# A squared-ReLU MLP kernel: small loads on other queues, transposes in merged PSUM banks, and a warm-up in four column tiles

## The chip, the cores and the metric

The kernel runs on one core of one Trainium2 chip. The metric is the device time of one execution in microseconds (us), as a median over several executions. "Span" is the time from the first to the last instruction in the profile; the device time is the span plus about 1.7 to 2.2 us. TensorE is called PE, its weight loads PEld, VectorE DVE, ScalarE ACT, GpSimd POOL, and SP is the engine that issues most DMAs.

## The reference

```python
B, S, D, F = 1, 2048, 576, 4608          # all bf16
def reference(x, w1, b1, w2, b2):
    h = jnp.einsum("bsd,df->bsf", x, w1) + b1
    r = jnp.where(h > zero, h, zero)
    h = r * r
    out = jnp.einsum("bsf,fd->bsd", h, w2) + b2
    return out
```

## The kernel before

The 2048 rows of x are worked in four blocks of 512. The first matmul contracts over D = 576, which is four full 128-row chunks and one of 64. The kernel deals with this in two ways. Four of the 36 column blocks of w1 ("w1n") are computed with full 128-row matmuls plus a 64-row pair ("w1n8"). The other 32 ("w_h" in the profile, w1_h in the code; when loaded, a piece of it is called a w1 chunk here) are computed as pairs of 64-row matmuls, one in the lower half of the array and one in the upper half, at the same time. I call this the row-tiled part.

x has to reach PE transposed. For blocks 1 to 3 a DMA transposes it; for block 0 there is no time for that, so PE transposes it into PSUM (the memory, divided into banks, that PE writes), and DVE and ACT copy it out, while full-array work on w1n is interleaved. Half 0 is the first 256 rows of the block, half 1 the rest. All of the change is in these first 10 us, the head. Cut to what matters (cuts are marked "# ..."):

```python
    # warm-up: matmuls on constants while the first loads fly
    WARM = [512] * 6 + [128]
    for i, n in enumerate(WARM):
        keep(nc.tensor.matmul(wps[:, 0:n], lhsT=ones[:, 0:P], rhs=ones[:, 0:n], start=True, stop=True))
    # ... loads: x tiles and w1n
    load_x(nc.sync, 0)
    load_x(nc.scalar, 1)
    load_w1n(nc.sync, 0)
    load_x(nc.scalar, 2)
    load_w1n(nc.sync, 1)
    load_x(nc.sync, 3)
    for k in range(2, NK):
        load_w1n(nc.sync, k)
    # ... b1 and b2's column by GpSimd
    nc.gpsimd.dma_start(out=b1_rows[0:NFT, :], in_=b1.rearrange("(ft p) -> ft p", p=P))
    # ... block 0: transposes, copies out of PSUM (DVE and ACT alternate), full-array matmuls
                for j in range(2):
                    for k in range(NK):
                        x_transpose(j, k)
                for j in range(2):
                    x_transpose(j, NK)
                x_copies(0)
                part(0, 0)
                for k in range(NK + 1):
                    x_transpose(2, k)
                part(0, 1)
                part(0, 2)
                for k in range(NK + 1):
                    x_transpose(3, k)
                x_copies(1)
                dup_windows(0)
                part(0, 3)
                part(1, 0)
                make_b1T()
                for k in range(1, NK):
                    part(1, k)
    # ... w1 for the row-tiled part, in the order in which it is needed
    for (j0, j1) in [(0, 1), (1, 2), (2, 4), (4, 6), (6, 8), (8, 10), (10, 12)]:
        load_w1(nc.sync, 0, j0, j1)
        load_w1(nc.sync, 1, j0, j1)
        if j0 == 0:
            load_w1n8(nc.sync, 0)
            load_w1n8(nc.sync, 1)
```

## Time and profile before

| | |
|---|---|
| time, median of 2 runs | 290.95 us (290.84 to 291.06) |
| span of the profiled run (a run of its own, 291.46 us) | 289.6 us; other runs of this kernel had 288.7 to 289.6 |
| PE busy | 285.5 us, 99% |
| row-tiled part starts | 9.85 us (first 64-row pair, which is w1n8's; counted from here below), 10.29 us (first w_h pair) |

The page of the kernel before: the first line gives each engine's busy time, the others the chain of work that ended last.

```profile
PE 285.5 (99%) x2027; PEld 139.9 (48%) x2032; DVE 78.6 (27%) x176; ACT 96.7 (33%) x154; POOL 2.3 (1%) x10
...
PE 98%; DMA 1%; issue 0%; DVE 0%
```

The kernel is PE from end to end, so only gaps in PE's work or slow PE work can be won back. The head, from the timeline of PE (columns: start us, length us, engine, line, operation, output<-inputs, forms, count, and in brackets an idle time before the first of them and what ended it):

```profile
0.78 2.83 PE L63 MATMUL wps<-const-bfloat16-1.0 128*128 128x512 bf16 x7 [0.78 <-PEq L344]
3.77 1.25 PE L149 MATMUL tb<-ident,x_sb 128*128 128x128 bf16 x10 [0.17 <-DMA x_sb<-in_x_dram]
4.87 1.01 PE L227 MATMUL pn<-xTw,w1n 128*128 128x256 bf16 x4
5.68 0.74 PE L149 MATMUL tb<-ident,x_sb 128*128 128x128 bf16 x5
6.21 1.19 PE L227 MATMUL pn<-xTw,w1n 128*128 128x256 bf16 x8
7.24 0.44 PE L149 MATMUL tb<-ident,x_sb 128*128 128x128 bf16 x5
7.51 1.04 PE L227 MATMUL pn<-xTw,w1n 128*128 128x256 bf16 x8
8.39 0.22 PE L166 MATMUL b1T_ps<-ident,b_rows 128*128 128x128 bf16 x1
8.44 1.47 PE L227 MATMUL pn<-xTw,w1n 128*128 128x256 bf16 x12
9.85 0.39 PE L203 MATMUL pn<-xTw,w1n 64*128 64x512 bf16 x1
```

From 3.77 us on, there is no gap. But the same work takes different times: four 256-column matmuls took 1.01 us at 4.87, and eight took 1.04 us at 7.51. PE's clock rises from half to full rate in between. The trace's own clock record puts the rise at 6.51 us in this run.

### The profile page before, as it was taken

The numbers are of one execution on the slowest core, as the hardware profiler recorded it, in microseconds if no ns is written. First come the engines' busy times: TensorE is split into PE (matmuls) and PEld (weight loads), VectorE is DVE, ScalarE is ACT, GpSimd is POOL, SyncE is SP. The second block draws the span as 40 slices with busy tenths as digits, with TensorE's granted clock in tenths as the row PEclk, the third lists the DMA queues.
The fourth block names the chain that finished last, engine by engine and source line by source line (L and its number), as shares of the span: only waits on it lengthen the run. The fifth ranks groups of instructions, "written<-read, shape, count | busy, mean of one in ns | idle before, by whom it ended". The sixth has DMA issues, their size and how long they took to land.

```text
span 289.6 us, 4693 instructions
## 1 busy us (share of the span) xinstructions
PE 285.5 (99%) x2027; PEld 139.9 (48%) x2032; DVE 78.6 (27%) x176; ACT 96.7 (33%) x154; POOL 2.3 (1%) x10
## 2 busy tenths in 40 slices
PE   8999999999999999999999999999999999999996
PEld 5544444444444555555544444444444455555555
DVE  1644554444500200000015444444440001100001
ACT  2566666666500000000027666666670000000000
POOL 3000000000000000000000000000000000000000
PEclk9999999999999999999999999999999999999999
DMA  7999999400001200000000000000000110000000
GB/s 198 221 245 188 308 389 212 92 0 2 0 14 25 52 16 18 16 16 18 16 16 2 1 2 0 2 0 2 0 2 0 36 38 16 16 16 19 33 16 18
DMA packets 31605, 16.52 MB, mean 57 GB/s; under 512 B 15700, under 2 KB 31584, under 8 KB 31584
## 3 DMA queue, kind: packets, MB, share of 16 engines
q1 hardware_dynamic: 31232, 15.91, 22.3%
q10 hardware_dynamic: 288, 0.30, 0.4%
q8 instruction: 16, 0.26, 0.4%
q14 instruction: 5, 0.04, 0.0%
q0 software_dynamic: 64, 0.01, 0.0%
HBM read 11.36 MB, written 2.36 MB: 47 GB/s over the span
## 4 chain that ended last, share of the span: by engine, by line
PE 98%; DMA 1%; issue 0%; DVE 0%
PE ph L188 42%; PE po L289 38%; PE pt L270 11%; PE pn L209 4%; PE pn L227 1%; DMA x_sb<-in_x_dram 1%; PE tb L149 1%; PE ph L190 1%; PE pn L203 1%; DVE o_sb L291 0%; PE b1T_ps L166 0%; PE pn L205 0%
## 5 line engine op out<-in xcount | busy, mean ns | idle before, releaser
L190 PE MATMUL ph<-xTw,w_h 64*128 64x512 bf16 x576 | 124.6, 376 | 0.0
L188 PE MATMUL ph<-xTw,w_h 64*128 64x512 bf16 x576 | 124.6, 376 | 0.0
L289 PE MATMUL po<-w_sb,hT 128*128 128x448 bf16 (+2 forms) x612 | 109.4, 341 | 0.0
L176 ACT ACTIVATE r<-ph,b1T 128x512 bf16<-128x512 f32 x128 | 81.1, 685 | 41.6 <-PE ph L190 41.6
L188 PEld LDWEIGHTS <-w_h 64*128 64x128 bf16 x576 | 54.1, 94 | 68.3
L289 PEld LDWEIGHTS <-hT 128*128 128x128 bf16 x612 | 58.5, 98 | 51.0
L177 DVE TENSOR_TENSOR hT<-r 128x512 bf16<-128x512 bf16 x144 | 61.2, 426 | 75.9 <-ACT r L176 75.5
L190 PEld LDWEIGHTS <-w_h 64*128 64x128 bf16 x576 | 54.1, 94 | 0.0
L291 DVE TENSOR_TENSOR o_sb<-po,b_bc 128x448 bf16<-128x448 f32 (+2 forms) x17 | 10.2, 597 | 125.8 <-PE po L289 125.8
L270 PE MATMUL pt<-hT,w_sb 128*128 128x512 bf16 x142 | 31.3, 379 | 0.1
L176 ACT ACTIVATE r<-pn,b1T 128x512 bf16<-128x512 f32 x16 | 10.3, 688 | 61.0 <-PE pn L205 59.6
L270 PEld LDWEIGHTS <-w_sb 128*128 128x128 bf16 x144 | 14.1, 98 | 17.0
L273 ACT ACTIVATE oT<-pt,b2T 128x512 bf16<-128x512 f32 x4 | 2.8, 688 | 28.3 <-PE pt L270 28.3
L209 PE MATMUL pn<-xTw,w1n 128*128 128x512 bf16 x45 | 10.4, 379 | 0.4 <-issue 0.3
L209 PEld LDWEIGHTS <-w1n 128*128 128x128 bf16 x48 | 4.5, 98 | 6.0 <-issue 0.8
L227 PE MATMUL pn<-xTw,w1n 128*128 128x256 bf16 x32 | 4.6, 295 | 0.0
L63 PE MATMUL wps<-const-bfloat16-1.0 128*128 128x512 bf16 (+1 forms) x7 | 2.8, 582 | 0.8 <-PEq L344 0.8
L227 PEld LDWEIGHTS <-w1n 128*128 128x128 bf16 x32 | 3.3, 107 | 0.5
L156 DVE COPY xTw<-tb 128x256 bf16<-128x256 bf16 x4 | 1.1, 292 | 6.7 <-PE tb L149 6.7
L119 DVE COPY xTw<-xTw 64x2048 bf16<-64x2048 bf16 x4 | 2.8, 690 | 0.2
L120 DVE COPY xTw<-xTw 64x2048 bf16<-64x2048 bf16 x4 | 2.7, 687 | 0.1
L149 PE MATMUL tb<-ident,x_sb 128*128 128x128 bf16 x20 | 2.4, 288 | 0.2 <-DMA x_sb<-in_x_dram 0.2
(23 smaller groups left out, 15.2 us busy)
## 6 DMA issues: line engine op xcount, KB each, us to landing
w_sb<-in_w_dram SPq DMA_DIRECT2D x4, 1296.0 KB, 12.7
w_h<-in_w_dram SPq DMA_DIRECT2D x14, 288.0 KB, 6.2
out_dram<-o_sb SPq DMA_DIRECT2D x15, 112.0 KB, 1.7
w_h<-in_w_dram SPq DMA_DIRECT2D x4, 144.0 KB, 3.5
w1n<-in_w_dram SPq DMA_DIRECT2D x4, 128.0 KB, 3.9
out_dram<-ot SPq DMA_DIRECT2D x4, 128.0 KB, 2.0
x_sb<-in_x_dram ACTq DMA_DIRECT2D x2, 144.0 KB, 2.9
x_sb<-in_x_dram SPq DMA_DIRECT2D x2, 144.0 KB, 3.4
```

The lines of the kernel that those rows point to most:

```text
L63: keep(nc.tensor.matmul(wps[:, 0:n], lhsT=ones[:, 0:P], rhs=ones[:, 0:n], start=True, stop=True))
L149: keep(nc.tensor.transpose(bank[:, slot, qc], xs[:, j, c0:c0 + P], ident[:]))
L176: keep(nc.scalar.activation(out=r[:], in_=bank[:], func=ACT.Relu, bias=b1T[:, ft:ft + 1], scale=1.0))
L177: keep(nc.vector.tensor_tensor(out=hTs[sb][:, ft, :], in0=r[:], in1=r[:], op=ALU.mult))
L188: keep(nc.tensor.matmul(bx[:], lhsT=w1_h[0:H, LO_C[i], jc], rhs=xT[0:H, LO_W[i], :], start=(i == 0), stop=(i == NC - 1)))
L190: keep(nc.tensor.matmul(by[:], lhsT=w1_h[H:P, UP_C[i], jc], rhs=xT[H:P, UP_W[i], :], start=(i == 0), stop=(i == NC - 1)))
L203: keep(nc.tensor.matmul(banks[2 * i][:], lhsT=w1n8[0:H, i, :], rhs=xT[0:H, SPC, :], start=start, stop=stop, skip_group_check=order == "k_o ...
L209: keep(nc.tensor.matmul(banks[g][:], lhsT=w1n[:, k, g * P:(g + 1) * P], rhs=xT[:, O + k, :], start=start, stop=stop))
L227: keep(nc.tensor.matmul(banks[g][:, hc], lhsT=w1n[:, k, g * P:(g + 1) * P], rhs=xT[:, O + k, hc], start=(h == 0 and k == 0), stop=False, s ...
L270: keep(nc.tensor.matmul(pt[:], lhsT=w2_sb[:, ft, DM:D], rhs=hT[:, ft, :], start=(i == 0), stop=(i == NFT - 1)))
L289: keep(nc.tensor.matmul(po[:, 0:d1 - d0], lhsT=hT[:, ft, jj * P:(jj + 1) * P], rhs=w2_sb[:, ft, d0:d1], start=(i == 0), stop=(i == NFT - 1)))
L291: keep(nc.vector.tensor_tensor(out=o_sb[:, d0:d1], in0=po[:, 0:d1 - d0], in1=b2_bc[:, d0:d1], op=ALU.add))
```

## The change

The intent is a shorter head: GpSimd out of the loads (b1, b2), b1 and the small w1 rows on ACT's queue so that SP can issue w1_h sooner, fewer and fuller PSUM banks for the transposes, and a warm-up of four matmuls at a time, each on 32 of the array's columns. The core of the diff:

```diff
-    WARM = [512] * 6 + [128]
-    for i, n in enumerate(WARM):
-        keep(nc.tensor.matmul(wps[:, 0:n], lhsT=ones[:, 0:P], rhs=ones[:, 0:n], start=True, stop=True))
+    CT = P // 4
+    WARM = [512] * 6 + [256]
+    for n in WARM:
+        for c in range(4):
+            keep(nc.tensor.matmul(wps[c * CT:(c + 1) * CT, 0:n], lhsT=ones[:, 0:CT], rhs=ones[:, 0:n],
+                                  start=True, stop=True))
 ...
     load_x(nc.sync, 0)
-    load_x(nc.scalar, 1)
-    load_w1n(nc.sync, 0)
-    load_x(nc.scalar, 2)
-    load_w1n(nc.sync, 1)
-    load_x(nc.sync, 3)
-    for k in range(2, NK):
-        load_w1n(nc.sync, k)
+    for rt in range(1, RT):
+        load_x(nc.scalar, rt)
+    for k0, k1 in [(0, 1), (1, 2), (2, NK)]:
+        load_w1n(nc.sync, k0, k1)
 ...  (the GpSimd loads of b1 and b2 go; ACT's table load and warm activation come here, then:)
+    for h in range(2):
+        load_w1n8(nc.scalar, h)
+    keep(nc.scalar.dma_start(out=b1_rows[0:NFT, :], in_=b1.rearrange("(ft p) -> ft p", p=P)))
 ...  (x_copies: half 0 all on DVE, half 1 on DVE with one double-width copy on ACT)
                 x_copies(0)
+                x_transpose(2)
                 part(0, 0)
-                for k in range(NK + 1):
-                    x_transpose(2, k)
                 part(0, 1)
-                part(0, 2)
-                for k in range(NK + 1):
-                    x_transpose(3, k)
+                x_transpose(3)
                 x_copies(1)
                 dup_windows(0)
+                part(0, 2)
                 part(0, 3)
 ...  (w1n8 leaves SP's queue; b2's column and w2 in three chunks instead of four come late on SP)
```

More of the change, by code (lines that the diff above doesn't have):

```diff
@@ L57 @@
     ps_o = ctx.enter_context(tc.tile_pool(name="ps_o", bufs=4, space=PSUM))
-    wps = ps_o.tile([P, 512], FP32, name="wps", tag="po")
+    wps = ps_h.tile([P, 512], FP32, name="wps", tag="ph")
     ones = nc.const_aps.tensor(1.0, [P, 512], BF16)
-    WARM = [512] * 6 + [128]
-    for i, n in enumerate(WARM):
-        keep(nc.tensor.matmul(wps[:, 0:n], lhsT=ones[:, 0:P], rhs=ones[:, 0:n], start=True, stop=True))
+    CT = P // 4
[4 more added lines that the diff above has]
+                                  start=True, stop=True))
     xs = const.tile([P, RT, D], BF16, name="x_sb")
@@ L72, in load_x, with load_w1n @@
         keep(eng.dma_start(out=xs[:, rt, :], in_=x2[rt * P:(rt + 1) * P, :]))
-    def load_w1n(eng, k):
-        keep(eng.dma_start(out=w1n[:, k, :], in_=w1[k * P:(k + 1) * P, 0:GW]))
+    def load_w1n(eng, k0, k1):
+        src = w1[k0 * P:k1 * P, 0:GW].rearrange("(k p) f -> p k f", p=P)
+        keep(eng.dma_start(out=w1n[:, k0:k1, :], in_=src))
     def load_w1n8(eng, h):
@@ L83, in load_w1 @@
                       in_=w1_v[:, :, GW + h * FH + j0 * P:GW + h * FH + j1 * P]))
+    b1_rows = const.tile([P, P], BF16, name="b1_rows")
+    nc.vector.memset(b1_rows[:], 0.0)
     load_x(nc.sync, 0)
-    load_x(nc.scalar, 1)
-    load_w1n(nc.sync, 0)
-    load_x(nc.scalar, 2)
-    load_w1n(nc.sync, 1)
-    load_x(nc.sync, 3)
-    for k in range(2, NK):
-        load_w1n(nc.sync, k)
+    for rt in range(1, RT):
+        load_x(nc.scalar, rt)
+    for k0, k1 in [(0, 1), (1, 2), (2, NK)]:
+        load_w1n(nc.sync, k0, k1)
     ident = const.tile([P, P], BF16, name="ident")
     make_identity(nc, ident[:])
-    b1_rows = const.tile([P, P], BF16, name="b1_rows")
-    nc.gpsimd.memset(b1_rows[:], 0.0)
-    nc.gpsimd.dma_start(out=b1_rows[0:NFT, :], in_=b1.rearrange("(ft p) -> ft p", p=P))
-    b2_col = const.tile([P, 1], BF16, name="b2_col")
-    nc.gpsimd.dma_start(out=b2_col[:], in_=b2[DM:D].rearrange("(d o) -> d o", o=1))
-    b2T = const.tile([P, 1], FP32, name="b2T")
-    nc.gpsimd.tensor_copy(out=b2T[:], in_=b2_col[:])
     warm = const.tile([P, 1], FP32, name="warm")
     keep(nc.scalar.activation(out=warm[:], in_=nc.const_aps.tensor(0.0, [P, 1], FP32), func=ACT.Relu))
+    for h in range(2):
+        load_w1n8(nc.scalar, h)
+    keep(nc.scalar.dma_start(out=b1_rows[0:NFT, :], in_=b1.rearrange("(ft p) -> ft p", p=P)))
     E3, O, SPC, E = 0, 1, 5, 6
@@ L130 @@
     w2_view = w2.rearrange("(ft p) d -> p ft d", p=P)
-    W2CH = 9
+    W2CH = 12
     def load_w2(c):
@@ L140, with x_transpose @@
     HS = SB // 2
-    tb_po = [ps_o.tile([P, 2, HS], BF16, name="tb", tag="po") for _ in range(2)]
-    tb_ph = [ps_h.tile([P, 2, HS], BF16, name="tb", tag="ph") for _ in range(4)]
-    half_banks = [tb_ph, None]
-    def x_transpose(j, k):
+    tb = [[ps_h.tile([P, 4, HS], BF16, name="tb", tag="ph") for _ in range(2)] for _ in range(2)]
+    PLACE = [(0, 0), (0, 1), (1, 0), (1, 1), (0, 2)]
+    T_ORDER = [0, 1, NK, 2, 3]
+    def x_transpose(j):
         h, q = divmod(j, 2)
-        qc = slice(q * P, (q + 1) * P)
-        bank, slot, c0 = (half_banks[h][k], 0, k * P) if k < NK else (half_banks[h][2], 1, D - P)
-        keep(nc.tensor.transpose(bank[:, slot, qc], xs[:, j, c0:c0 + P], ident[:]))
+        for k in T_ORDER:
+            bank, slot = PLACE[k]
+            c0 = k * P if k < NK else D - P
+            keep(nc.tensor.transpose(tb[h][bank][:, slot, q * P:(q + 1) * P], xs[:, j, c0:c0 + P], ident[:]))
     def x_copies(h):
         hc = slice(h * HS, (h + 1) * HS)
-        for k in range(NK):
-            src = half_banks[h][k][:, 0, :]
-            if k % 2 == 0:
-                keep(nc.vector.tensor_copy(out=xT0[:, O + k, hc], in_=src))
-            else:
-                keep(nc.scalar.copy(out=xT0[:, O + k, hc], in_=src))
-        keep(nc.vector.tensor_copy(out=xT0[:, E3, hc], in_=half_banks[h][2][:, 1, :]))
+        for k in (0, 1):
+            keep(nc.vector.tensor_copy(out=xT0[:, O + k, hc], in_=tb[h][0][:, k, :]))
+        if h == 0:
+            for k in (2, 3):
+                keep(nc.vector.tensor_copy(out=xT0[:, O + k, hc], in_=tb[h][1][:, k - 2, :]))
+        else:
+            keep(nc.scalar.copy(out=xT0[:, O + 2:O + 4, hc], in_=tb[h][1][:, 0:2, :]))
+        keep(nc.vector.tensor_copy(out=xT0[:, E3, hc], in_=tb[h][0][:, 2, :]))
     b1T = const.tile([P, NFT], FP32, name="b1T")
     def make_b1T():
-        b1T_ps = ps_o.tile([P, P], BF16, name="b1T_ps", tag="po")
+        b1T_ps = ps_h.tile([P, P], BF16, name="b1T_ps", tag="ph")
         keep(nc.tensor.transpose(b1T_ps[:], b1_rows[:], ident[:]))
@@ L198, in a_full @@
         for g in range(G):
-            pool, tag = (ps_o, "po") if g < 2 else (ps_h, "ph")
+            pool, tag = (ps_o, "po") if g < 2 or order == "k_outer" else (ps_h, "ph")
             banks.append(pool.tile([P, SB], FP32, name="pn", tag=tag))
@@ L220, in a_full @@
             if order == "k_outer":
-                tb_new = [ps_h.tile([P, 2, HS], BF16, name="tb", tag="ph") for _ in range(2)]
-                half_banks[1] = tb_new + tb_po
                 def part(h, k):
@@ L231, in a_full @@
                 for j in range(2):
-                    for k in range(NK):
-                        x_transpose(j, k)
-                for j in range(2):
-                    x_transpose(j, NK)
+                    x_transpose(j)
                 x_copies(0)
+                x_transpose(2)
                 part(0, 0)
-                for k in range(NK + 1):
-                    x_transpose(2, k)
                 part(0, 1)
-                part(0, 2)
-                for k in range(NK + 1):
-                    x_transpose(3, k)
+                x_transpose(3)
                 x_copies(1)
                 dup_windows(0)
+                part(0, 2)
                 part(0, 3)
@@ L296 @@
         load_w1(nc.sync, 1, j0, j1)
-        if j0 == 0:
-            load_w1n8(nc.sync, 0)
-            load_w1n8(nc.sync, 1)
     load_xT(1)
@@ L303 @@
         load_w1(nc.sync, 1, j0, j1)
+    b2_col = const.tile([P, 1], BF16, name="b2_col")
+    keep(nc.sync.dma_start(out=b2_col[:], in_=b2[DM:D].rearrange("(d o) -> d o", o=1)))
+    b2T = const.tile([P, 1], FP32, name="b2T")
+    nc.gpsimd.tensor_copy(out=b2T[:], in_=b2_col[:])
     keep(nc.sync.dma_start(out=b2_bc[:], in_=b2.partition_broadcast(P)))
-    for c in (0, 2, 1, 3):
+    for c in range(3):
         load_w2(c)
```

## The prediction

> **What bounds it now.** TensorE. The profile's first table has PE busy 285.5 of 289.6 us (99%), and the chain of waits is 98% PE; only x_sb's first load (about 3 us) and the last store lie outside it. From about 10.3 us to 287 us PE issues 512-column matmuls every 0.215 us without gaps, and the diff leaves that part alone (w2 in three chunks instead of four is needed only at 77 us). So only the first 10.3 us can change.
>
> **The head, from the timeline.** Warm-up matmuls start at 0.78 us, 0.427 us apart (half clock), and end near 3.6; x tile 0 lands at 3.72; the transposes start at 3.77; from there PE is dense to the first row-tiled pair at 9.85. In this stretch PE waits for data only 0.2 us. The clock is still low for its first part: 128-column transposes start 0.107 us apart and 256-column matmuls 0.213 us apart until about 6.5 us, then 0.055 and 0.109. At full rate the 21 transposes and 32 matmuls would take 21x0.055+32x0.109 = 4.6 us instead of 6.1. So the most that the head can give is about 1.4 us, 0.5%, and it can be had only by an earlier clock, since PE has no gaps to close.
>
> **What the change does.**
> - GpSimd loads and memset go (POOL is busy 2.3 us, off the chain): worth 0.
> - b1_rows and the small w1 rows move to ScalarE's queue, behind three x issues (0.43 us each), the table load (1.28) and the warm activation (0.2): b1 is issued near 5 us and lands, at the 2.5 to 3.5 us of loads in this stretch, near 7.5 to 8.5. PE's b1 transpose came at 8.39. Just in time; if the clock rises early, a stall of 0 to 0.7 us.
> - Merged banks: half 0's five copies now all run on DVE, 0.29 us each. The first needs the bank's eighth transpose, but five transposes of tile 2 (0.53 us) fill that wait. About 0.
> - w1n chunks 2 and 3 in one load, issued near 2.1 instead of 2.65 us: needed at about 7; no wait, unless PE is earlier.
> - Warm-up as four column tiles. The Trainium skill, "TensorE: Matmul & The Clock Gate", Part 3, reports three column tiles running 2.38 times as fast as in sequence, so I take four as concurrent: the trace already shows the two 64-row tiles starting within 0.01 us of each other. Then the warm-up ends about where it did, 3.6 to 3.9 us. The same page, Part 1, has the clock rise after a busy free-running window of about 3.4 us; the trace agrees loosely (activity from 0.78, rise at 6.5). Four times as many matmuls in a window may count as more activity and raise the clock one window earlier (about 30% by my guess): gain 0.7 to 1.3 us, less the stalls above. Otherwise 0, or a loss of 0.1 to 0.3 us for the drain at the mode switch and the longer last warm-up.
>
> **Predicted: 290.6 us** (0.3*(-1.0) + 0.7*(-0.05), about -0.35), 8 times in 10 between 289.7 and 291.5. Faster by over 2%: 0.01; within 2%: 0.97; slower: 0.02.
>
> **What would show it.** Right: four warm-up matmuls start within some 0.02 us of each other; first transpose at 3.7 to 3.9; the rows part starts between 9 and 10.4 us; its length and everything after unchanged to 0.3 us. Clock: the step at which starts of 256-column matmuls halve their distance, 6.5 before.
>
> **What would make it wrong.** Column tiles run one after the other: 28 warm-up matmuls then last till about 9 us, and the kernel takes some 295 us. Or b1_rows lands after 9 us and PE stalls at its transpose. Or the window's phase differs between executions, and moves either kernel by up to 1 us.

## The result, and the profile after

The changed kernel took 291.24 us (median of 2 runs, 291.12 and 291.35) against 290.95. The ratio is 1.0009, with a 95% interval of 0.9985 to 1.0033. Ratios here are the mean time of one kernel's fast runs over that of the other's of the same rounds, so they are not quite the ratio of the medians quoted. The page and PE's timeline after:

```profile
PE 285.9 (99%) x2053; PEld 155.7 (54%) x2053; DVE 78.8 (27%) x179; ACT 95.9 (33%) x151; POOL 0.9 (0%) x7
...
PE 99%; DVE 0%; issue 0%
```

```profile
0.77 2.96 PE L65 MATMUL wps<-const-bfloat16-1.0 128*32 128x512 bf16 x28 [0.77 <-PEq L337]
3.67 1.78 PE L149 MATMUL tb<-ident,x_sb 128*128 128x128 bf16 x15
5.24 1.35 PE L224 MATMUL pn<-xTw,w1n 128*128 128x256 bf16 x8
6.43 0.44 PE L149 MATMUL tb<-ident,x_sb 128*128 128x128 bf16 x5
6.71 1.47 PE L224 MATMUL pn<-xTw,w1n 128*128 128x256 bf16 x12
8.02 0.22 PE L166 MATMUL b1T_ps<-ident,b_rows 128*128 128x128 bf16 x1
8.08 1.47 PE L224 MATMUL pn<-xTw,w1n 128*128 128x256 bf16 x12
9.48 0.39 PE L203 MATMUL pn<-xTw,w1n 64*128 64x512 bf16 x1
```

The 28 column-tile matmuls end about when the seven old ones did, so four of them do run at once. The row-tiled part starts at 9.48 instead of 9.85 us. This looks like a gain of 0.37 us, but two sums show where it comes from.

**Sum 1, the head.** Count the work from the first transpose to the row-tiled part, with cold time counted half. Before: (6.51 - 3.77)/2 + (9.85 - 6.51) = 4.71 us. After, with the clock rise at 5.88 us in the trace's record: (5.88 - 3.67)/2 + (9.48 - 5.88) = 4.71 us. PE has the same work and no gap in either. So the row-tiled part starts at 4.71 us plus half of (first transpose + clock rise), and nearly all of the 0.37 us is a clock that happened to rise 0.64 us earlier (0.32) plus a first transpose 0.10 us earlier (0.05).

**Sum 2, the rest.** Before, 289.60 - 9.85 = 279.75 us remain after the head; after, 289.31 - 9.48 = 279.83. The rest is unchanged but for some 0.1 us. That 0.1 us has a place: in the changed kernel the upper of two w_h matmuls that otherwise start together came late, and in the kernel before it did not (from the two timelines, after and before):

```profile
13.81 0.38 PE L188 MATMUL ph<-xTw,w_h 64*128 64x512 bf16 x1
13.96 0.39 PE L190 MATMUL ph<-xTw,w_h 64*128 64x512 bf16 x1
...
14.18 0.38 PE L188 MATMUL ph<-xTw,w_h 64*128 64x512 bf16 x1
14.18 0.38 PE L190 MATMUL ph<-xTw,w_h 64*128 64x512 bf16 x1
```

The chunk that it needs landed at 13.91 us; tiles_alone below shows a stronger case.

The window of 0 to 14 us in the DMA view shows one thing that I had not looked for. Before (columns: queue and kind, packets, MB, share of 16 engines' time):

```profile
q1 hardware_dynamic: 5810, 2.62, 75.6%
q10 hardware_dynamic: 288, 0.30, 8.2%
q0 software_dynamic: 64, 0.01, 0.4%
```

After:

```profile
q1 hardware_dynamic: 5372, 2.41, 71.0%
q10 hardware_dynamic: 768, 0.52, 12.6%
q8 instruction: 1, 0.02, 0.6%
```

The GpSimd queue (q0) is gone and ACT's (q10) has grown, as meant. New in this window is a q8 "instruction" packet of 16 KB. The records of the trace have it at 15.4 us before and at 11.4 us after. The experiments make it matter.

### The profile page after: what moved, and what is told of

It reads as the page before. It is cut to its first block, busy times and chain, and to the rows that moved or that the text cites. A ratio compares the mean times of both kernels' runs of the same rounds, so it can differ in the third digit from the quotient of the medians.

```text
span 289.3 us, 4738 instructions
## 1 busy us (share of the span) xinstructions
PE 285.9 (99%) x2053; PEld 155.7 (54%) x2053; DVE 78.8 (27%) x179; ACT 95.9 (33%) x151; POOL 0.9 (0%) x7
## 4 chain that ended last, share of the span: by engine, by line
PE 99%; DVE 0%; issue 0%
PE po L281 38%; PE ph L188 28%; PE ph L190 15%; PE pt L262 11%; PE pn L209 4%; PE pn L224 1%; PE wps L65 1%; PE tb L149 1%; PE pn L203 1%; PE pn L205 0%; DVE o_sb L283 0%; PE b1T_ps L166 0%
## 5 line engine op out<-in xcount | busy, mean ns | idle before, releaser
L176 ACT ACTIVATE r<-pn,b1T 128x512 bf16<-128x512 f32 x16 | 10.3, 687 | 61.5 <-PE pn L205 60.0
L65 PE MATMUL wps<-const-bfloat16-1.0 128*32 128x512 bf16 (+1 forms) x28 | 3.0, 598 | 0.8 <-PEq L337 0.8
L203 PE MATMUL pn<-xTw,w1n 64*128 64x512 bf16 x8 | 2.4, 379 | 0.0
L205 PE MATMUL pn<-xTw,w1n 64*128 64x512 bf16 x8 | 2.4, 379 | 0.0
## 6 DMA issues: line engine op xcount, KB each, us to landing
w_sb<-in_w_dram SPq DMA_DIRECT2D x3, 1728.0 KB, 12.6
```

The lines of the kernel that those rows point to most:

```text
L65: keep(nc.tensor.matmul(wps[c * CT:(c + 1) * CT, 0:n], lhsT=ones[:, 0:CT], rhs=ones[:, 0:n], start=True, stop=True))
L176: keep(nc.scalar.activation(out=r[:], in_=bank[:], func=ACT.Relu, bias=b1T[:, ft:ft + 1], scale=1.0))
L203: keep(nc.tensor.matmul(banks[2 * i][:], lhsT=w1n8[0:H, i, :], rhs=xT[0:H, SPC, :], start=start, stop=stop, skip_group_check=order == "k_o ...
```

## The experiments

The theories, as they stood before the first eight runs. A: PE is dense, and what is left is the phase of a clock grid that the kernel does not control. B: four matmuls at a time count as more activity and raise the clock earlier. C: the parts each move something, and cancel. Theory D came from the traces of those eight: the larger number of PE instructions brings forward the fetch of instructions, which delays a w1 chunk. All kernels gave correct results. Ratios are to the kernel before in the same rounds.

Four readings of each profiled run. "Rule" is 4.71 us + half of (first transpose + rise), or first transpose + 4.71 where the rise came earlier. "w1 chunk" is the one of w1_h for column blocks 2 and 3, upper half: when the last of its 16 shares landed, by the trace's records, and when PE wanted it (first w_h pair + 18 pairs of 0.2155 us). A dash: not read.

| run | median us | ratio (95%) | clock rise | rule | row-tiled part starts | first fetch | w1 chunk landed / wanted |
|---|---|---|---|---|---|---|---|
| before | 290.95 | | 6.51 | 9.85 | 9.85 | 15.4 | 13.16 / 14.17 |
| the change | 291.24 | 1.0009 (0.9985, 1.0033) | 5.88 | 9.48 | 9.48 | 11.4 | 13.91 / 13.81 |
| after_again | 291.24 | 1.0027 (1.0004, 1.0049) | 4.26 | 8.67 | 9.67 | 11.7 | 13.99 / 13.99 |
| no_warm | 292.59 | 1.0060 (1.0048, 1.0072) | 9.55 | 11.30 | 11.25 | 17.0 | - |
| one_tile | 291.25 | 1.0014 (1.0002, 1.0026) | 6.40 | 9.72 | 9.71 | 13.1 | 12.58 / 14.04 |
| tiles_alone | 292.01 | 1.0034 (1.0021, 1.0047) | 5.37 | 9.23 | 9.39 | 11.5 | 15.06 / 13.72 |
| full_array_warm | 291.12 | 1.0009 (0.9997, 1.0022) | 3.45 | 8.35 | 9.52 | 13.5 | 12.78 / 13.84 |
| loads_alone | 292.26 | 1.0052 (1.0033, 1.0071) | 4.80 | 8.88 | 10.36 | 16.0 | - |
| banks_and_tiles | 292.05 | 1.0038 (1.0025, 1.0052) | 4.39 | 8.74 | 8.92 | 11.2 | 14.78 / 13.24 |
| dma_half | 292.38 | 1.0075 (1.0036, 1.0114) | 13.39 | - | 13.53 | 18.1 | - |
| count_alone | 291.76 | 1.0034 (1.0019, 1.0050) | 6.74 | 9.94 | 9.93 | 12.3 | 13.10 / 14.25 |
| lead_tiles | 291.35 | 1.0016 (1.0002, 1.0031) | 5.18 | 9.14 | 9.69 | 11.5 | 14.96 / 14.01 |
| banks_alone | 290.63 | 0.9990 (0.9977, 1.0002) | 4.5 to 4.8 | 8.8 to 8.9 | 9.05 | 15.6 | 13.39 / 13.4 |
| banks_lead | 290.95 | 1.0002 (0.9989, 1.0015) | 3.69 | 8.29 | 10.00 | 15.7 | 13.08 / - |

("First fetch" is the start of the first q8 packet. For banks_alone the clock record is missing; the rise is read from where the starts of matmuls halve their distance.) Where the start equals the rule, PE had no gap in the head. Where it is later, PE waited for data there. The idle times in brackets in the timelines count from the modelled end of the matmul before, so they are shorter than the time lost from start to start.

### after_again: the changed kernel, once more

> The changed kernel once more, unaltered, for a tight interval. Theory A (phase of the clock): from the first transpose PE has no gaps, so the row-tiled part starts at 4.71 us of full-rate work plus half of (clock rise + first transpose); the rise falls on a 3.41 us grid that the kernel's start does not control, anywhere from 4.2 to 7.6 us for a warm-up that begins at 0.78 us. Then the ratio to before is 1.000, within 0.998 to 1.002, and single runs of either kernel differ by up to 1.7/2 us. Theory B (the count): four matmuls at a time count as more activity and raise the clock a window earlier on average; then the ratio is 0.996 to 0.998. Theory C (cancelling parts): the loads or the banks gain something that another part loses; the ratio is 1.000 too, but the parts alone will differ.

No edit. The ratio came out above the range that theory A gave: 1.0027, with an interval clear of 1. Its six runs had spans of 288.8, 289.3, 289.4, 289.5, 290.9 and 291.1 us; those of before, in the same rounds, 288.7 to 289.6. So the change costs 0.1 to 0.3%, part of it in two single long runs (290.9 and 291.1) of which there is no trace; what those two met is open. The trace of one run shows another thing: the clock rose early, at 4.26 us, and PE could not use it.

```profile
5.88 0.45 PE L149 MATMUL tb<-ident,x_sb 128*128 128x128 bf16 x5
6.71 1.48 PE L224 MATMUL pn<-xTw,w1n 128*128 128x256 bf16 x12 [0.38 <-DMA w1n<-in_w_dram]
8.20 0.23 PE L166 MATMUL b1T_ps<-ident,b_rows 128*128 128x128 bf16 x1
```

PE waits for w1n chunks 2 and 3, which now come as one load. By the rule it could have been 1.0 us earlier. An early clock moves the limit from PE to the loads.

### no_warm: the changed kernel without the warm-up

```diff
-    for n in WARM:
-        for c in range(4):
-            keep(nc.tensor.matmul(wps[c * CT:(c + 1) * CT, 0:n], ...))
```

> The changed kernel without warm-up matmuls; first PE activity is then the transposes at 3.7 us. Theory A: the rise comes 2.9 us later than with a warm-up, between 7.1 and 10.5 us; the row-tiled part starts at 10.1 to 11.8 us instead of 9.1 to 10.4; the time is longer by 1.0 to 1.9 us, ratio 1.0035 to 1.0065. If warm-up bought nothing (a rival for why its form doesn't matter), ratio 1.000 and a rise as before, 5.9 to 6.5 us.

Ratio 1.0060, inside the range given by theory A; rise at 9.55 us, start of the row-tiled part at 11.25 against 11.30 by the rule.

```profile
3.63 1.78 PE L141 MATMUL tb<-ident,x_sb 128*128 128x128 bf16 x15 [3.63 <-DMA x_sb<-in_x_dram]
5.20 1.91 PE L216 MATMUL pn<-xTw,w1n 128*128 128x256 bf16 x8
```

Eight 256-column matmuls take 1.91 us, all cold. At the medians a warm-up is worth 1.35 us against the changed kernel, from which this run differs by the warm-up alone, and 1.7 us against the kernel before. So the form of the warm-up could have mattered.

### one_tile: a quarter of the array

```diff
-        for c in range(4):
+        for c in range(1):
```

> The changed kernel with only one of the four column tiles in the warm-up: 7 matmuls of 32 columns over the same time, a quarter of the array at work. Theory A (busy time counts, not array use): rise between 4.2 and 7.6 us, ratio to before 0.998 to 1.002. Theory B (the amount of work counts): a quarter of the work is too little, the rise comes as without a warm-up, 7.1 to 10.5 us, ratio 1.0035 to 1.0065.

Ratio 1.0014, inside theory A's range and clear of no_warm's 1.0060: a quarter of the columns does nearly all that a warm-up does for the time. The rise came at 6.40 us, but this one rise proves little: of the 3.41 us before it, only 0.7 us were warm-up (it ended at 3.70), the rest the transposes and matmuls that every kernel has. For theory B, that four tiles raise the clock earlier, nothing speaks here, nor in the next run.

### tiles_alone: the kernel before with the four column tiles

```diff
-    WARM = [512] * 6 + [128]
-    ... one full-array matmul each
+    WARM = [512] * 6 + [256]
+    ... four 32-column matmuls each
```

> The kernel before with the warm-up as four column tiles, nothing else changed. Theory A: ratio 0.998 to 1.002, warm-up still ends at 3.6 to 3.8 us, four matmuls start within 0.02 us of each other. Theory B: rise earlier than before's 6.5 us, at 3.1 to 4.5, and ratio about 0.997. Theory C: ratio off 1.000 in the direction opposite to the loads and banks.

Nothing of this held for the time: the ratio is 1.0034, all five runs (spans 289.8 to 290.5) above all eleven of before (288.7 to 289.6). The warm-up itself was as expected, and the clock rose at 5.37 us, earlier than in the profile of before. The loss is elsewhere. (Theory C doesn't hold either: the loads lose too when alone, see loads_alone.) PE's timeline of this run at 13 to 15 us:

```profile
13.51 0.38 PE L193 MATMUL ph<-xTw,w_h 64*128 64x512 bf16 x1
13.72 0.38 PE L191 MATMUL ph<-xTw,w_h 64*128 64x512 bf16 x1
15.11 0.39 PE L193 MATMUL ph<-xTw,w_h 64*128 64x512 bf16 x1 [1.01 <-DMA w_h<-in_w_dram]
```

Pairs come every 0.2155 us, so the upper half's matmul should have started beside the lower one at 13.72: 1.39 us lost. With the rest of Sum 2, 9.39 + 279.75 + 1.39 = 290.5 us, which is the span. The wait is for a chunk of w1, and the records of its 16 shares (each DMA engine reports its share) show how it came late, here beside the same chunk in the kernel before:

```
              first   8th    14th   15th   last share landed (us)
before        12.06   12.65  12.95  12.99  13.16
tiles_alone   12.04   12.52  13.08  13.24  15.06
```

Fifteen shares came in time, one 1.8 us after. In front of it stands the q8 packet. The DMA view of tiles_alone in the window 11.5 to 13 us:

```profile
q1 hardware_dynamic: 732, 0.36, 112.1%
q8 instruction: 1, 0.02, 4.8%
```

One packet of 16 KB (16,384 bytes in the record) took 1.16 us. One share of this 288 KB chunk is 18 KB (288/16), so, as an estimate from the sizes, a DMA engine that has to move the packet falls behind by about a whole share. The Trainium skill describes such a queue ("Runtime: NRT & Kernel Launch", section "Instruction fetch mechanics"): an engine's instructions are refilled in 16 KiB blocks of 256 instructions over a DMA queue that its sequencer drives, and the cost is "mostly hidden". The trace agrees with the size, and with the pace: in the kernel before the first two packets are 12.6 us apart, during which PE starts 235 instructions, and its 16 packets would hold 4096 instructions, where the trace has 4065 matmuls and weight loads of PE. It was not hidden here.

The four-tile warm-up has 28 matmuls and 28 weight loads instead of seven of each: 42 more PE instructions. They are used up in the warm-up, and this fits a first fetch that comes sooner: in the records PE had started 150 instructions after its warm-up when the fetch began, against 214 in the kernel before. (The number isn't constant: 146 to 158 in the six normal runs with 56 warm-up instructions, 174 to 234 in the seven with 14 or none; dma_half, with its long waits on PE, had 178. What sets it within these ranges is open.) That is 11.5 instead of 15.4 us, where w1 still lands just ahead of PE.

That the late share sits on the same DMA engine as the fetch is argued; the records do not name the engine. But all 14 traces have the same pattern. No w1 chunk that landed before the first fetch had a last share more than 0.54 us behind the 15th. With the first, second or third chunk to finish after the fetch began, one share falls 0.7 to 1.8 us behind, and it stays so for several chunks. The kernel before has this too: its fetch comes at 15.4 us, and the chunk whose other shares landed by 17.95 us was complete at 18.97. There PE wanted that chunk only at 21.9 us (first w_h pair + 54 pairs), so it cost nothing. By this pattern an early fetch does not create the delay; it moves it to where w1 has no time to spare.

### full_array_warm: the changed kernel with the old warm-up

```diff
-    WARM = [512] * 6 + [256]  (four column tiles)
+    WARM = [512] * 6 + [128]  (full array)
```

> The changed kernel with the old warm-up (seven matmuls on the full array). Theory A: ratio to before 0.998 to 1.002, rise between 4.2 and 7.6 us. Theory B: rise later on average than with four tiles, ratio 0.002 to 0.004 above that of the changed kernel.

Ratio 1.0009, as expected by theory A, so the new loads and banks together are not worth anything either. The clock rose at 3.45 us, earlier than I thought possible and before the first transpose. By the rule the row-tiled part could start at 8.35; it started at 9.52. Two of the waits:

```profile
4.57 0.45 PE L146 MATMUL tb<-ident,x_sb 128*128 128x128 bf16 x5 [0.19 <-DMA x_sb<-in_x_dram]
...
8.05 0.23 PE L163 MATMUL b1T_ps<-ident,b_rows 128*128 128x128 bf16 x1 [0.28 <-DMA b_rows<-in_b_dram]
```

This is the stall for b1 that the prediction named for an early clock. The fetch came at 13.5 us, and the chunk was in time.

### loads_alone: the kernel before with the new queues alone

```diff
-    ... x1, x2 on ACT, x3 on SP; w1n in four loads; b1, b2 on GpSimd; w1n8 on SP
+    ... x1 to x3, w1n8, b1 on ACT; w1n in three loads; b2's column late on SP; w2 in three chunks
```

> The kernel before with the new queues and order of the loads alone (no GpSimd loads, b1 and the small w1 rows on the ScalarE queue, w1n chunks 2 and 3 in one load, w2 in three chunks); transposes, banks and warm-up as before. ScalarE's copies of x now stand behind the issues of the small loads on ScalarE (last one ends near 5.9 us; the first ScalarE copy was at 4.63). Theory A: matmul order gives PE nothing to fill that wait, so PE idles up to 1.2 us and the kernel is slower by 0.5 to 1.2 us, ratio 1.002 to 1.004; this would be why the copies of half 0 were moved to VectorE. Theory C with a gain from loads: ratio below 0.999.

Slower, ratio 1.0052, above the range that I gave, for the reason that I gave. PE and ACT:

```profile
4.63 0.55 PE L223 MATMUL pn<-xTw,w1n 128*128 128x256 bf16 x3
6.33 0.27 PE L223 MATMUL pn<-xTw,w1n 128*128 128x256 bf16 x1 [1.14 <-ACT xTw L154]
```

```profile
3.67 1.35 ACTq L80 DMA_DIRECT2D w1n<-in_w_dram  x2
5.12 0.74 ACTq L100 DMA_DIRECT2D b_rows<-in_b_dram  x1
5.90 0.65 ACT L154 COPY xTw<-tb 128x256 bf16<-128x256 bf16 x2 [2.26 <-DVE xTw L155]
```

ACT's copies of x now come after the issue of the small loads, at 5.90 us instead of 4.63, and PE sits idle. The move of half 0's copies to DVE in the same change is what makes the new queues bearable.

### banks_and_tiles: the changed kernel with the old loads

```diff
-    ... the new loads
+    ... the loads of the kernel before (b1, b2 on GpSimd, w1n8 on SP, x3 on SP)
```

> The changed kernel with the old loads (GpSimd loads b1 and b2, SP loads the small w1 rows, x tile 3 on SP). Theory A: PE dense, row-tiled part at 4.71 plus half of (rise + first transpose), ratio 0.998 to 1.002. Theory C: ratio off 1.000 by 0.002 or more.

Ratio 1.0038, the same loss as tiles_alone, at the same place: PE waits from 13.24 us to 14.82 for the same chunk (1.58 us lost), whose last share landed at 14.78 and the 15th at 13.72. The first fetch came at 11.2 us.

### dma_half: an attempt to beat both, from the changed kernel

```diff
-    for rt in range(1, RT):
-        load_x(nc.scalar, rt)
-    ... w1n on SP; transposes and copies of half 1 on PE and DVE/ACT
+    load_x(nc.scalar, 1)
+    keep(nc.sync.dma_start_transpose(out=xT0[:, 1:1 + NK, HS:SB], in_=x2[HS:SB, 0:P * NK]))
+    keep(nc.sync.dma_start_transpose(out=xT0[:, 0:1, HS:SB], in_=x2[HS:SB, D - P:D]))
+    ... w1n on ACT; half 1 needs no transposes or copies
```

> An attempt to beat both: rows 256 to 511 of block 0 are transposed by DMA on the SP queue instead of loaded and transposed by TensorE; w1n moves to the ScalarE queue. Removes 10 of 20 transposes, 10 x 0.055 = 0.55 us of full-rate PE work (1.1 us at the low clock), and five copies. The estimate is a row-tiled part that starts 0.3 to 0.8 us earlier for the same rise, ratio 0.997 to 0.9985, if the DMA transposes land before about 7 us (their landing took 4.0 us elsewhere in the profile) and PE does not wait for the first copy without the five transposes that filled that wait (a gap of 0.3 us expected). If the transposes land late, PE stalls and the ratio is 1.000 or above.

It lost, ratio 1.0075. PE's timeline:

```profile
5.09 1.01 PE L225 MATMUL pn<-xTw,w1n 128*128 128x256 bf16 x4 [0.17 <-DVE xTw L155]
6.86 1.03 PE L225 MATMUL pn<-xTw,w1n 128*128 128x256 bf16 x4 [0.76 <-DMA w1n<-in_w_dram]
8.26 3.59 PE L225 MATMUL pn<-xTw,w1n 128*128 128x256 bf16 x16 [0.37 <-DMA w1n<-in_w_dram]
```

w1n came late: its second chunk was issued at 1.67 us, as in the kernel before, but landed at 6.81 instead of 5.86 us. That the DMA transposes held it up is argued, since w1n also changed its queue. PE was idle in the gaps, and the clock rose only at 13.39 us in this run; that the gaps delayed the rise is likely, not shown. Of its six runs two had spans above 293 us and four 290.0 to 290.8; even those are slower than before. The missing transposes on PE are worth less than prompt w1n.

### count_alone: many short full-array matmuls

```diff
-    WARM = [512] * 6 + [128]
+    WARM = [112] * 28
```

> The kernel before with 28 short full-array warm-up matmuls (112 columns) in place of seven long ones: the instruction count of the four-tile warm-up, but no column tiling, in about the same time. Theory D (new, from the traces of the first eight runs): the 42 extra TensorE instructions bring forward the first fetch of TensorE's instructions, one 16 KB transfer of about 1.2 us on one DMA engine, from 15.4 us to about 11.5; there it delays that engine's share of the w1 chunk that PE needs at about 13.8 us, and PE waits about 1 us. Then: fetch at 11 to 12 us, one of the chunk's 16 shares lands over 1 us after the 15th, PE idles 0.5 to 1.3 us on w_h, ratio 1.002 to 1.0045 as with the column tiles (1.0034). Rival E (column tiling itself, by its mode or its reads, slows something): ratio 1.000, no wait on w_h.

No column tiling, same number of instructions as tiles_alone, same ratio: 1.0034. So the loss does not need column tiling, which speaks for the number and against rival E. The trace of the one profiled run is a partial miss. Its clock rose late (6.74 us), the fetch came at 12.3 us, one share of the next chunk was late (15 landed by 14.27 us, the last at 15.84), but PE was not there yet and had no wait; its span of 289.7 us is what the head alone gives (9.93 + 279.75). The other four runs had spans of 289.8, 290.0, 290.1 and 290.8. Before's nine runs of the same rounds ended at 289.4. Waits in those four are inferred, not seen. A late clock alone would hardly do it: 6.74 us is the latest rise in any trace with a warm-up but dma_half's, it belongs to this run, and the four are 0.1 to 1.1 us longer.

### lead_tiles: the tiles, with the small w1 rows out of SP's way

```diff
+    ... the four-tile warm-up, as in tiles_alone
+    for h in range(2):
+        load_w1n8(nc.scalar, h)      # behind x tile 2, ahead of ACT's table load
-        if j0 == 0:
-            load_w1n8(nc.sync, 0)
-            load_w1n8(nc.sync, 1)
```

> The kernel before with the four-tile warm-up and with the small w1 rows issued on the ScalarE queue right behind x tile 2, ahead of ScalarE's table load, so that the w1 chunks leave SP 1.3 us earlier and ScalarE's copies still find their time. Theory D: the fetch still comes at 11 to 12 us and still delays one share, but the chunk has 1.3 us more lead; the wait on w_h falls from 1.0 us to 0 to 0.3, ratio 1.000 to 1.0015. Rival E: the ratio stays at 1.0034.

The ratio fell from 1.0034 to 1.0016, about as expected, but the profiled run does not show why. In it the chunk landed at 14.96 us (the 15th share at 13.50), and PE lost 1.00 us (the upper matmul started at 15.01 instead of 14.01). That run was the slowest of the five (290.4; the others 289.2 to 289.6). Nor did the edit give the lead that it was meant to give: in this run SP issued the chunk at 8.61 us, not earlier but later than in tiles_alone (8.38), because SP's queue itself had to wait twice for a load of x before it could issue (from the waits of SP, 0 to 10 us; total us, times, longest):

```profile
SPq L78 <- DMA x_sb<-in_x_dram: 1.0, 1, 1.0
SPq L85 <- DMA x_sb<-in_x_dram: 0.7, 1, 0.7
```

The kernel before has no such wait. So the lead as I explained it is not shown, and the lower ratio has no shown cause. What makes the whole change lose less than its tiles alone stays partly open. In its two profiled runs SP issued this chunk at 8.06 and 7.86 us (SP's queue waits for loads there too, 2.1 us in the first), the other shares had landed by 12.8 and 12.6 us, and the last at 13.9 to 14.0, when PE was just asking; which of the moves brought that forward was not separated.

### banks_alone: merged banks and the new order alone

```diff
-    ... ps_o/ps_h half banks, copies on DVE and ACT alternately, transposes of tile 2 after part(0, 0)
+    ... four merged banks, half 0's copies on DVE, transposes of tile 2 before part(0, 0)
```

> The kernel before with the merged banks, the new order of transposes and the VectorE copies alone; old loads, old warm-up. Theory D: fetch back at 13 to 15.5 us, no wait or under 0.3 us on w_h, ratio 0.998 to 1.001; the 1.0038 of banks and tiles together is then the tiles' share. If the banks cost something of their own, ratio 1.002 or more.

Ratio 0.9990, interval 0.9977 to 1.0002; median 290.63 us, the lowest of all. The five spans lie between 288.7 and 289.1. Its median is 0.6 us below the changed kernel's, though of other rounds; against before it is not clear of noise.

### banks_lead: banks alone plus the small w1 rows early on ACT

```diff
+    for h in range(2):
+        load_w1n8(nc.scalar, h)      # behind x tile 2; no longer on SP
```

> An attempt to beat both: merged banks, old full-array warm-up, b1 and b2 by GpSimd as before, small w1 rows on the ScalarE queue right behind x tile 2. PE has neither the ScalarE wait nor the early fetch, and w1 has 1.3 us more lead. Theory D: no wait on w_h, no wait for b1; ratio 0.998 to 1.0005; it can gain on before only where before waited for w1 after an early clock rise, so at most some 0.3 us.

Ratio 1.0002, not better than banks alone. The clock rose at 3.69 us, and PE then waited 0.94 us for w1n, so that the row-tiled part started at 10.00 us; nothing waited for w_h or b1. The lead was small here too: the chunk was issued at 7.96 us, 0.43 us earlier than in the kernel before and not 1.3.

## Why the prediction was right or wrong

The time was inside the range (290.6 predicted, 289.7 to 291.5; measured 291.24), and "within 2%" was right. Part of this is luck: the forecast was a gain of 0.35 us, what was measured is a loss of 0.29, and in after_again two of six runs (292.69 and 292.87) lie above the range. The reasons held in part.

- **PE bounds the kernel: right. "Only the first 10.3 us can change": too narrow.** The prediction took the steady part as safe because the diff leaves its matmuls alone. But its data can come late: PE lost 1.00 to 1.58 us at 13 to 15 us in the three runs named next, and some 0.1 us in the changed kernel. In all 14 profiled runs the span is the start of the row-tiled part plus 279.75 us plus PE's loss on w1 (1.39 us in tiles_alone, 1.58 in banks_and_tiles, 1.00 in lead_tiles, else 0.1 or none), to within 0.1 us. (Example: full_array_warm 9.52 + 279.75 = 289.27, measured 289.20.)
- **"It can be had only by an earlier clock, since PE has no gaps to close": half right.** The rule shows it for runs with a late clock. But in the three runs with a rise before 4.3 us (after_again, full_array_warm, banks_lead) PE waited for w1n, x or b1 instead, and the row-tiled part still started at 9.5 to 10.0 us. The earliest start in any trace is 8.92 us, so the 1.4 us that I put as the most were not to be had with these loads.
- **Four tiles run at once and end at about the same time: right.** 28 matmuls in 2.96 us against seven in 2.83.
- **"Four times as many matmuls in a window may count as more activity" (30%, up to 1.3 us of gain): no run supports it.** Rises were spread from 3.45 to 6.74 us in the kernels with a warm-up, whatever its form (dma_half, with its gaps, left out); with four tiles they came at 4.26 to 5.88, with the full array at 3.45 to 6.74. This was the term that pulled the forecast to a gain.
- **The cost of the warm-up's form, "0, or a loss of 0.1 to 0.3 us for the drain at the mode switch": wrong in cause and size.** Alone it costs 1.1 us at the median (292.01 against 290.90 in its rounds). In the profiled run the wait for the late w1 share, 1.39 us, accounts for it, and count_alone, with as many instructions and no mode to switch, has the same ratio; its own waits were not seen.
- **b1 just in time, a stall if the clock rises early: right.** No wait in the profiled run, 0.28 us of PE idle in full_array_warm.
- **w1n chunks in one load, "no wait, unless PE is earlier": right**, 0.38 us in after_again.
- **"Merged banks: about 0": right**, ratio 0.9990 with 1 in the interval. What I missed is that DVE's copies are what the new queues need; without them the queues alone cost 1.14 us of PE idle time.
- **GpSimd's loads worth 0:** not tried by themselves.
- **"The window's phase differs between executions": right** (the clock of the changed kernel rose at 5.88 us in one run and at 4.26 in another), and it is why one profile each would have misled: it showed the changed kernel 0.3 us faster when it is 0.1 to 0.3% slower.

## What to carry to other kernels

First account for each profile with a sum (here: start of the steady part, plus a constant, plus stalls), and correct for what differs between executions, before you credit a change with a few tenths of a microsecond. Count instructions as well as work: on a stream that is fed just in time, extra instructions on one engine can move its instruction fetches, and in these runs the last sixteenth of the loads that followed a 16 KB fetch came 0.7 to 1.8 us late. Check also that an edit did what it was meant to do: lead_tiles was to issue a load 1.3 us earlier, and its trace has it 0.2 us later. Parts of a change that add up to nothing can each cost something alone, so keep those that help (here the banks, at most) rather than the whole.

## What the Trainium skill lacked or had wrong

- "Runtime: NRT & Kernel Launch", section "Instruction fetch mechanics", calls the cost of crossing a block "mostly hidden". In tiles_alone a 16,384-byte fetch of 1.16 us at 11.5 us came before a w1 chunk whose last share landed 1.8 us after the 15th, and PE lost 1.39 us. No page says how far such a fetch sets back the loads that are under way; here it was 0.7 to 1.8 us in all 14 traces.
- "TensorE: Matmul & The Clock Gate", Part 1, has a free-running window of 3413 ns, and the traces agree: the record of full clock in the kernel before lasts 283.306 us, which is 83.0 such windows (82.0, 83.0 or 84.0 in the other 12 runs with a record). But it has the rise after a busy window without saying how busy. In full_array_warm it rose at 3.45 us with PE active from 0.78, 78% of the window; in the kernel before it did not rise one window ahead of 6.51, at 3.10 us, with 68%. So part of a window can be enough. But the timeline's busy share alone does not give a threshold: there was no rise with 73% in no_warm (at 6.14 us) and 75% in count_alone (at 3.33), but none either in dma_half at 9.98 us, with 81% of the window before it busy by the modelled ends of the matmuls.
- The same page, Part 4, says that the full clock "doesn't engage" for transpose mode. Here the kernel calls nc.tensor.transpose, the trace lists matmuls, and the starts of these 128-column transposes are 0.107 us apart before the rise and 0.055 us apart after it, so they run at the full clock once it is there. Whether transposes count towards the rise is not shown.
- No page says whether a matmul on part of the array's columns counts for as much in the clock gate as one on all. In after_again the clock rose at 4.26 us after 3.41 us of which 2.9 were the four-tile warm-up; with one tile the ratio to before was 1.0014, without a warm-up 1.0060. That four tiles count for more, no run shows.
